# Two routing batches in place of three, the first tile's products around the last routing chain, scores in the first PSUM banks, and a thinner word-decoding schedule in the second expert

## The chip, the cores and the metric

The kernel runs on one core of a Trainium2 chip. The metric is the device time of one launch in microseconds (us); lower is better. The core has a matrix engine (PE, with its weight loads as PEld), a vector engine (DVE), an activation engine (ACT), a general engine (POOL, called GpSimd in the code) and a queue engine that issues most transfers (SP). Each engine works through its own instructions in order. PE writes to eight PSUM banks, which DVE and ACT read.

## What is computed

Sliding-window attention with four sink positions (2 sequences, 8 heads, 768 positions, width 64) gives 1536 rows of 512. A router picks two of eight experts for each row, a two-layer expert network runs on the rows of each expert, and a dense two-layer network with a sigmoid gate follows.

```python
x = attention(q, k, v)                              # 1536 x 512
noisy = x @ w_gate + log1p(exp(x @ w_noise)) * noise
top2 = the two largest of the 8 noisy logits of a row; weights = softmax of the two
out[mask] += weight * (relu(x[mask] @ w1[e]) @ w2[e])     # for each expert e
h = out @ w_in;  result = (h * sigmoid(h)) @ w_out        # w_in, w_out come as 64-bit floats
```

## The kernel before

**Numbers.** Each matrix product is made of three half-precision products (high by high, high by low, low by high). So each operand needs a high part (ACT, or POOL for the first weights) and a low part (DVE, the helper `low`, line 126).

**Attention** runs as a pipeline over steps p = 0 to 59. Steps 0 to 47 each begin the scores of a pair of heads of one block of 128 rows (four steps a block, 12 blocks); their later stages follow one to five steps behind. Work is hung on the steps by `at(step, function)`, and each engine's order is the order in which these functions are called. Per step DVE takes a maximum of the scores (`mx`, line 473) and a low part (`plo`, line 504). For each block the rows are scaled (`xs`, line 563), stored, transposed (`pm`, line 203), multiplied by the router's weights (`pl`, line 212) and copied to `lg` (line 215).

**Routing** of a batch of blocks (`noisy_top`, `route`) is a list of small steps, most of them on DVE, called the drip: a step of the attention takes one from it in its middle and one at its end, and four at its end from step 48 on. It ends in one-hot matrices `Aoh` and `Boh`, whose product (`z_part`, line 763) lists for each slot of an expert the row that goes there (`idx`, line 813). `posm` (lines 277 to 281) counts the rows ahead on PE. There are three batches: blocks 0 to 4, 5 to 8 and 9 to 11.

**The first tile.** Once the first batch is routed, the first 128 rows of expert 0 are known. They are gathered (`f_list`, line 668) and taken through expert 0 on their own: transposed (`f_xt`, line 675), first layer (`f_l1`, 24 matmuls, line 682), `f_relu`, transposed (`f_ht`, line 692), second layer (`f_l2`, 24 matmuls, line 699), out (`f_out`, line 704). The list `work` holds these as pieces, and `do_fill` runs the next ones at chosen places of the end of the attention. After `idx`, `f_gather` (line 717) fetches the other three tiles of expert 0 and `f_rows` (lines 727 and 729) transposes and splits them into `xT`.

**Experts** (`moe`): for expert e, eight pieces f of the first layer (`l1`, line 1009) alternate with the second (`l2`, line 1025). Beside them, for the next expert, rows are gathered by POOL (line 980), split (line 988) and turned by a DMA transpose on SP (`x_turn`, line 1369, one at each of f = 3 to 6 from the second expert on). `weights_step` loads and splits 512 KB weight pieces (line 877), two at each f in the second expert. `decode_step` decodes the 64-bit words of the dense network in 67 steps: an even one takes the last operation of one piece, ACT and POOL work on the next (lines 936, 937) and a load of 512 KB (line 931); an odd one stores a decoded 256 KB piece (line 962) and has two DVE operations.

Of the kernel before, what the change touches and what calls it, by code (L numbers as in the profile page):

```python
# [22 lines left out]
BATCHES = ((0, 5), (5, 9), (9, 12))  # L23
# [21 lines left out]
def setup(ctx, tc, g):  # L45
    nc = tc.nc
# [24 lines left out]
    g.iota8 = consts.tile([128, 8], F32, name="iota8")  # L71
    g.M = consts.tile([128, g.NB, 8], BF16, name="M")
    g.Msum = consts.tile([128, 8], BF16, name="Msum")
    g.top8 = consts.tile([128, g.NB, 8], F32, name="top8")
    g.ix = consts.tile([128, g.NB, 8], U32, name="ix")
    g.ef = consts.tile([128, g.NB, 2], F32, name="ef")
# [17 lines left out]
def setup_ops(tc, g):  # L94
# [3 lines left out]
    nc.gpsimd.iota(g.iota8, pattern=[[1, 8]], base=0, channel_multiplier=0,  # L98
                   allow_small_or_imprecise_dtypes=True)
    nc.gpsimd.iota(g.iotaq, pattern=[[1, 128]], base=0, channel_multiplier=0,  # L100
# [119 lines left out]
def noisy_top(tc, g, t, j0, j1):  # L220

    nc = tc.nc
    n = j1 - j0
    J = slice(j0, j1)
    V = nc.vector
    e, u, l, z, dd = (t("r" + c, [8]) for c in "eulzd")
    pre, nz = t("rp", [8]), t("rn", [8])
# [12 lines left out]
    add(lambda: V.tensor_scalar(z, u, 1.0, None, op0=OP.is_equal))  # L240
    add(lambda: V.scalar_tensor_tensor(dd, u, 1.0, z, op0=OP.subtract, op1=OP.add))
    add(lambda: V.tensor_mul(e, e, g.noise_sb[:, J, :]))
    add(lambda: V.reciprocal(dd, dd))
    add(lambda: V.tensor_mul(z, z, e))
    add(lambda: V.tensor_mul(dd, dd, e))
    add(lambda: V.tensor_add(pre, z, g.lg[:, J, 0:8]))
    add(lambda: V.tensor_mul(l, l, dd))
    add(lambda: V.tensor_add(nz, l, pre))
# [4 lines left out]
    return st  # L253


def route(tc, g, wk, ps, j0, j1):
# [6 lines left out]
    def t(name, shape, dt=F32):  # L263
# [3 lines left out]
    pos = t("rpos", [2])  # L267
    sl, pm, cl = (t(c, [2], I32) for c in ("rsl", "rpm", "rcl"))
    st = noisy_top(tc, g, t, j0, j1)
    add = st.append  # L270
    add(lambda: V.tensor_tensor(oh, g.iota8[:, None, None, :].to_broadcast([128, n, 2, 8]),
                                g.ix[:, J, 0:2, None].to_broadcast([128, n, 2, 8]), op=OP.is_equal))
    add(lambda: V.tensor_add(g.M[:, J, :], oh[:, :, 0, :], oh[:, :, 1, :]))

    def posm():
        p = ps.tile([128, n, 8], F32, name="pp", tag="M")
        nc.tensor.matmul(p, g.tri, g.M[:, J, :], start=True, stop=n == 1 and j0 == 0)
        if j0:
            nc.tensor.matmul(p, g.ones, g.Msum[:, None, :].to_broadcast([128, n, 8]), start=False, stop=n == 1)
# [5 lines left out]
        if j1 == g.NB:  # L285
            g.do_fill(4)
        V.tensor_copy(g.ef[:, J, :], g.ix[:, J, 0:2])
# [4 lines left out]
    add(lambda: V.tensor_reduce(pos, ps2, axis=AX.X, op=OP.add))  # L292

    add(lambda: V.scalar_tensor_tensor(sl, g.ef[:, J, :], 512.0, pos, op0=OP.mult, op1=OP.add))
# [12 lines left out]
    add(lambda: V.scalar_tensor_tensor(g.sl[:, J, :], g.ef[:, J, :], float(g.C), pos, op0=OP.mult, op1=OP.add))  # L307
    if j1 < g.NB:
        tot = wk.tile([128, 8], F32, name="rtot", bufs=1)

        def msum():
            V.tensor_reduce(tot, g.M[:, J, :].rearrange("p j e -> p e j"), axis=AX.X, op=OP.add)
            if j0:
                V.tensor_add(tot, tot, g.Msum)
            V.tensor_copy(g.Msum, tot)
# [5 lines left out]
def attention(tc, g):  # L321
# [4 lines left out]
    with ExitStack() as st:  # L326
# [241 lines left out]
        keep_warm(nc, g, ps, "O", 10)  # L568
# [43 lines left out]
        for n in range(NQ):  # L612
# [20 lines left out]
            if n == NQ - 1:  # L633
                at(e + 5, lambda: do_fill(2))
            at(e + 6, ga[3], "dve0")
        at(4, lambda: setup_ops(tc, g))
        for j0, j1 in g.batches:
            at(4 * j1 + (8 if j0 else 10), lambda j0=j0, j1=j1: drip.extend(route(tc, g, wk, ps, j0, j1)))
            if j0 == 0:
                at(4 * j1 + 10, lambda: drip.append(f_begin))  # L640
            if j1 == g.batches[-1][0]:
                at(4 * j1 + 8, lambda j1=j1: drip.append(lambda: z_part(0, j1)))
# [9 lines left out]
        def f_split(k, scale):  # L652
# [3 lines left out]
            nc.scalar.activation(hi, p, AF.Copy, scale=scale)  # L656
# [45 lines left out]
        def f_out():  # L702
# [6 lines left out]
        work = (fl[0] + fl[1][:2] + [lambda: f_relu(0)] + fl[1][2:] + [lambda: f_ht(0), lambda: f_relu(1)] + f2[0][:2]  # L709
                + [lambda: f_ht(1)] + f2[0][2:] + f2[1] + [f_out])  # L710
# [32 lines left out]
        g.do_fill = do_fill  # L743
# [29 lines left out]
        for p in range(NP + 12):  # L773
# [30 lines left out]
            if p == 52:  # L804
                f_xt()
            if p >= 57:
# [8 lines left out]
        do_fill(len(fill) - 5)  # L815
        f_rows(1)
        f_rows(2)
        do_fill(1)
        f_rows(3)
        do_fill(len(fill))  # L820
# [149 lines left out]
def moe(tc, g, W, wk, ps):  # L970
# [98 lines left out]
    def gates():  # L1069
# [8 lines left out]
            lambda: V.tensor_sub(e2, g.top8[:, :, 1], g.top8[:, :, 0]),  # L1078
# [68 lines left out]
    for i, (e, f) in enumerate(seq):  # L1147
# [39 lines left out]
        if i == 7:  # L1187
            dec[0][0]()
            dec[1][0]()

        for _ in range((0, 1, 1, 1, 1, 1, 2, 2)[f] + (f == 4 and e % 2) if e else 0):
# [197 lines left out]
def flag_steps(tc, g, wk, ps):  # L1389
# [3 lines left out]
    t = wk.tile([128, 5], F32, name="flt", bufs=1)  # L1393
# [3 lines left out]
    def count():  # L1397
        p = ps.tile([128, 13], F32, name="pc", tag="PT")
        nc.tensor.matmul(p[:, 0:8], g.ones, g.Msum, start=True, stop=False, skip_group_check=True)
        for j in range(g.batches[-1][0], g.NB):  # L1400
            nc.tensor.matmul(p[:, 0:8], g.ones, g.M[:, j, :], start=False, stop=False, skip_group_check=True)
        nc.tensor.matmul(p[:, 8:13], g.ones, g.over, start=False, stop=True, skip_group_check=True)
        V.tensor_reduce(t[:, 0:1], p[:, 0:8], axis=AX.X, op=OP.max)
# [6 lines left out]
            lambda: V.tensor_scalar(t[:, 0:1], t[:, 0:1], float(g.C), None, op0=OP.is_gt),  # L1410
            lambda: V.tensor_scalar(t[:, 4:5], t[:, 4:5], 0.5, None, op0=OP.is_gt),
# [28 lines left out]
def general(tc, g):  # L1440
# [4 lines left out]
    with ExitStack() as ctx:  # L1445
# [72 lines left out]
        with ExitStack() as st:  # L1518
# [15 lines left out]
            for f in noisy_top(tc, g, t, 0, NB):  # L1534
                f()
# [122 lines left out]
```

## Time and profile before

| | |
|---|---|
| median of 3 runs | 711.97 us (711.9 to 711.98) |
| profiled execution | 713.08 us, of which the span from the first to the last instruction is 711.4 us |
| mean granted TensorE clock | 0.982 of full speed |
| busy share of the span | PE 94%, DVE 60%, ACT 47%, POOL 30% |
| steps of the attention, up to the first product of expert 0 | 0 to 154.34 us |
| experts | 154.34 to about 445 us |
| dense network | to 711.4 us |

The profiled execution is 1.1 us longer than the median of the runs. Times in the text below are microseconds from the start of the span. PE is the busiest engine, so what counts is where it waits and where it ran at the lower of its two clocks.

### The profile page before, as it was taken

To read this page: it belongs to the slowest core of one execution; us is meant where nothing else is said; L and a number is where in the kernel's file an instruction comes from. 1 tells how busy PE (TensorE), PEld (TensorE's weight loads), DVE (VectorE), ACT (ScalarE), POOL (GpSimd) and SP (SyncE) were. 2 spreads that over 40 slices of the span, in tenths; PEclk is the share of its full clock that TensorE was granted. 3 is DMA by queue.
4 is the path that set the end of the run, shared out by engine and by line. 5 is a ranking of instruction groups with operands and counts; after the bars stand their busy time and mean duration, and the time that the engine had idled before them with its cause. 6 is when DMAs were issued, how large, how long until landed. Compare 5 with 4: busy or idle time off the path is not lost.

```text
span 711.4 us, 11618 instructions
## 1 busy us (share of the span) xinstructions
PE 667.1 (94%) x4292; PEld 373.1 (52%) x4292; DVE 429.3 (60%) x1091; ACT 337.8 (47%) x693; POOL 214.2 (30%) x229
## 2 busy tenths in 40 slices
PE   7999889889987999999999999899999999999993
PEld 5677667557543656565555553444444444444441
DVE  5878788737695687878797854756423344232222
ACT  4888868437663555556555441443323223222221
POOL 5868950142162162625252325222100000000000
PEclk9999999799998999999999999999999999999998
DMA  7776710539798989998894514742311011000001
GB/s 153 197 168 178 179 46 24 186 97 242 283 253 309 236 293 270 330 276 267 232 297 155 150 45 135 241 149 67 82 30 59 1 30 29 30 30 1 1 0 65
DMA packets 111682, 103.50 MB, mean 145 GB/s; under 512 B 77312, under 2 KB 77568, under 8 KB 111616
## 3 DMA queue, kind: packets, MB, share of 16 engines
q1 hardware_dynamic: 106016, 86.68, 42.4%
q0 software_dynamic: 4096, 13.11, 6.1%
q10 hardware_dynamic: 1504, 2.88, 1.1%
q8 instruction: 35, 0.57, 0.3%
q14 instruction: 31, 0.25, 0.1%
HBM read 77.29 MB, written 17.30 MB: 133 GB/s over the span
## 4 chain that ended last, share of the span: by engine, by line


## 5 line engine op out<-in xcount | busy, mean ns | idle before, releaser
L1009 PE MATMUL ph<-xT,w 128*128 128x416 f16 (+1 forms) x768 | 141.7, 335 | 8.8 <-DMA win_d<-f 6.6
L1274 PE MATMUL p<-xT,w 128*128 128x512 f16 x576 | 132.2, 379 | 2.1 <-DVE xT L1260 1.4
L1291 PE MATMUL po<-w,h 128*128 128x512 f16 x576 | 132.2, 379 | 0.0
L1025 PE MATMUL py<-h,w 128*128 128x416 f16 (+1 forms) x672 | 124.1, 331 | 3.2 <-DVE h L131 2.7
L937 POOL TENSOR_SCALAR f<-f 128x512 f32<-128x512 f32 x32 | 70.6, 2211 | 157.7 <-ACT f L936 155.6
L1009 PEld LDWEIGHTS <-w 128*128 128x128 f16 x768 | 75.4, 98 | 61.3 <-DMA win_d<-f 7.0
L1277 DVE TENSOR_TENSOR f<-p,f 128x512 f32<-128x512 f32 x48 | 33.1, 691 | 110.9 <-ACT f L1276 109.3
L1025 PEld LDWEIGHTS <-w 128*128 128x128 f16 x672 | 65.7, 98 | 52.6 <-issue 6.1
L1274 PEld LDWEIGHTS <-w 128*128 128x128 f16 x576 | 56.4, 98 | 70.1 <-issue 2.4
L1291 PEld LDWEIGHTS <-h 128*128 128x128 f16 x576 | 56.3, 98 | 67.8 <-DVE h L126 0.3
L1276 ACT ACTIVATE f<-p 128x512 f32<-128x512 f32 x48 | 28.6, 596 | 128.8 <-PE p L1274 126.5
L1012 ACT ACTIVATE h<-ph 128x416 f16<-128x416 f32 (+1 forms) x64 | 31.8, 497 | 52.0 <-PE ph L1009 51.0
L126 DVE SCALAR_TENSOR_TENSOR h<-f,h 128x512 f16<-128x512 f32 x48 | 33.2, 692 | 33.4 <-ACT h L1279 33.4
L126 DVE SCALAR_TENSOR_TENSOR w<-wst,w 128x1024 f16<-128x1024 f32 x38 | 47.2, 1245 | 8.4 <-ACT w L882 8.1
L131 DVE SCALAR_TENSOR_TENSOR h<-ph,h 128x416 f16<-128x416 f32 (+1 forms) x64 | 36.2, 566 | 24.3 <-ACT h L1012 24.3
L1279 ACT ACTIVATE h<-f 128x512 f16<-128x512 f32 x48 | 30.2, 629 | 37.8 <-DVE f L1277 37.8
L482 ACT ACTIVATE P<-pS,mx 128x260 f32<-128x260 f32 (+1 forms) x96 | 43.0, 458 | 1.9 <-DVE mx L473 1.6
L882 ACT ACTIVATE w<-wst 128x1024 f16<-128x1024 f32 x38 | 39.6, 1047 | 0.0
L126 DVE SCALAR_TENSOR_TENSOR rows<-xg,rows 128x512 f16<-128x512 f32 (+1 forms) x36 | 24.8, 688 | 24.2 <-ACT rows L988 24.1
L980 POOL DMA_INDIRECT xg<-x_d,idx x28 | 32.6, 1166 | 20.5 <-DVE topsl L121 13.5
L1064 ACT ACTIVATE yo<-tpy 128x512 f32<-128x512 f32 (+1 forms) x27 | 16.1, 595 | 45.4 <-PE tpy L1054 29.6
L126 DVE SCALAR_TENSOR_TENSOR w<-rows,w 128x1024 f16<-128x1024 f32 x26 | 31.9, 1231 | 4.4 <-ACT w L882 4.1
(254 smaller groups left out, 956.1 us busy)
## 6 DMA issues: line engine op xcount, KB each, us to landing
wst<-in_moe_w_dram SPq DMA_DIRECT2D x42, 512.0 KB
rows<-in_moe_w_dram SPq DMA_DIRECT2D x22, 512.0 KB
f<-in_moe_w_in_dram SPq DMA_DIRECT2D x16, 512.0 KB
f<-in_moe_w_out_dram SPq DMA_DIRECT2D x16, 512.0 KB
y_d<-yo SPq DMA_DIRECT2D x23, 256.0 KB
rawv<-in_v_dram SPq DMA_DIRECT2D x12, 256.0 KB
x_d<-xs SPq DMA_DIRECT2D x12, 256.0 KB
rows<-in_k_dram SPq DMA_DIRECT2D x11, 256.0 KB
```

Of the source, the lines that this page charges most:

```text
L126: nc.vector.scalar_tensor_tensor(o, x, scale, hi, op0=OP.mult, op1=OP.subtract, accum_out=sum_at(g)[:o.shape[0]] if check else None)
L131: nc.vector.scalar_tensor_tensor(o, x, 0.0, hi, op0=OP.max, op1=OP.subtract, accum_out=sum_at(g))
L482: nc.scalar.activation(Pt[n][:, h, :wd], psS[pr][:, a, :wd], AF.Exp, bias=nmx[pr][:, a:a + 1], accum_out=sm[n][:, h:h + 1])
L882: nc.scalar.activation(self.u[u][k][0][:, 2 * h:2 * h + 2, :], st["t"], AF.Copy, scale=scale)
L937: nc.gpsimd.tensor_scalar(a, a, 2.0 ** -15, 2.0 ** -80, op0=OP.max, op1=OP.mult)
L980: nc.gpsimd.indirect_dma_start(out=t[:CT[c]], out_offset=None, in_=g.x_d[:, :], in_offset=bass.IndirectOffsetOnAxis(ap=g.idx[:CT[c], 4 * e ...
L1009: nc.tensor.matmul(p[:, v], w[x][:, d, c], xT[e][y][:, d, v], start=d == 0 and k == 0, stop=d == 3 and k == 2)
L1012: nc.scalar.activation(hi[:, v], p[:, v], AF.Relu)
L1025: nc.tensor.matmul(ys[e][d][:, v], w[x][:, f % 4, d * 128:(d + 1) * 128], h[y][:, v], start=f == 0 and k == 0, stop=f == 7 and k == 2)
L1274: nc.tensor.matmul(p, w[x][:, d, c], xT[q][y][:, d, :], start=z == 0, stop=z == 11)
L1277: V.tensor_mul(s, p, s)
L1291: nc.tensor.matmul(po[q][t], h[x][:, 128 * t:128 * t + 128], w[y][:, f % 4, :], start=f == 0 and k == 0, stop=f == 15 and k == 2)
```

## The change

It does five things.

1. The routing batches become blocks 0 to 5 and 6 to 11. The first enters the drip at step 34 (it was 30), the last at step 55 (it was 56).
2. The routing is written with fewer DVE operations: the two largest logits are found for a whole batch by two reductions and comparisons, in place of a `max` and a `max_index` for each block; slot numbers start from preset counts in `Msum`; the `z` term of the logarithm goes.
3. The first tile's work moves: its list at step 48, `f_xt` at step 56, five pieces at step 57 and five at step 59, its second layer after the gathers are issued. Its first high part is taken by DVE and no longer by ACT. `f_rows` and `f_out` come last, in that order.
4. The warm-up tile takes the tag "S", so the scores' tiles get the first PSUM banks. The expert stage takes its first two banks for `ph`, the output of `l1`.
5. In the second expert `decode_step` runs once at each of f = 1 to 7 (it was 10 steps, now 7), and ten times in each later one (it was 9 or 10).

```diff
-BATCHES = ((0, 5), (5, 9), (9, 12))
+BATCHES = ((0, 6), (6, 12))
...
-    t = ps.tile([128, 4, 128], F32, name="warm", tag=tag)
+    t = ps.tile([128, 2, 512], F32, name="warm", tag=tag)[:, 0].rearrange("p (a b) -> p a b", a=4)
...
-    for j in range(n):
-        add(lambda j=j: V.max(g.top8[:, j0 + j, :], nz[:, j, :]))
-    for j in range(n):
-        add(lambda j=j: V.max_index(g.ix[:, j0 + j, :], g.top8[:, j0 + j, :], nz[:, j, :]))
...
+    def pick(k):
+        m = g.top2[:, J, k]
+        add(lambda: V.tensor_reduce(m, nz, axis=AX.X, op=OP.max))
+        add(lambda: V.tensor_tensor(oh[:, :, k, :], nz, m[:, :, None].to_broadcast([128, n, 8]), op=OP.is_equal))
+    pick(0)
+    add(lambda: V.scalar_tensor_tensor(nz, oh[:, :, 0, :], -3e38, nz, op0=OP.mult, op1=OP.add))
+    pick(1)
...
-        if j1 == g.NB:
-            g.do_fill(4)
...
-        keep_warm(nc, g, ps, "O", 10)
+        keep_warm(nc, g, ps, "S", 10)
...
-                at(e + 5, lambda: do_fill(2))
+                at(e + 7, lambda: f_xt())
+                at(e + 8, lambda: do_fill(5))
+                at(e + 10, lambda: do_fill(5))
...
-            nc.scalar.activation(hi, p, AF.Copy, scale=scale)
+            if k:
+                nc.scalar.activation(hi, p, AF.Copy, scale=scale)
+            else:
+                nc.vector.tensor_scalar(hi, p, scale, None, op0=OP.mult)
...
+        do_fill(len(fill))
+        f_ht(0)
         z_part(g.batches[-1][0], NB)
         z = zt[0]
         nc.vector.tensor_scalar(g.idx, z, float(g.N - 1), None, op0=OP.min)
         f_gather()
-        do_fill(len(fill) - 5)
+        for f in f2[0][:2] + [lambda: f_ht(1)] + f2[0][2:] + f2[1]:
+            f()
+        for f in g.after:
+            f()
         f_rows(1)
         f_rows(2)
-        do_fill(1)
         f_rows(3)
-        do_fill(len(fill))
+        f_out()
...
-        for _ in range((0, 1, 1, 1, 1, 1, 2, 2)[f] + (f == 4 and e % 2) if e else 0):
+        for _ in range(((0, 1, 1, 1, 1, 1, 1, 1), (0, 1, 1, 1, 1, 2, 2, 2))[e > 1][f] if e else 0):
             decode_step(dstep[0])
```

On PE, at the very end of the attention, these rows stood before: the transposes of two of the fetched tiles (`rawv`), then the second layer of the first tile (`pf_2744`), with the third tile's transposes nine matmuls ahead of the first product of expert 0 (`ph`, not shown here).

```order
L699 LDWEIGHTS fp_204
L699 MATMUL pf_2744<-w_377,fp_204 128x512
L727 MATMUL pf_2765<-idf,rawv 128x128 x4
L727 MATMUL pf_2772<-idf,rawv 128x128 x4
L699 LDWEIGHTS fp_203
L699 MATMUL pf_2744<-w_1136,fp_203 128x512
```

In the changed kernel, at the same place, up to the first product of expert 0:

```order
L707 LDWEIGHTS fp_202
L707 MATMUL pf_2671<-w_1135,fp_202 128x512
L734 MATMUL pf_2706<-idf,rawv 128x128 x4
L734 MATMUL pf_2713<-idf,rawv 128x128 x4
L734 MATMUL pf_2720<-idf,rawv 128x32 x4
L1016 LDWEIGHTS w_374
L1016 MATMUL ph<-xT,w_374 128x288
```

All three tiles' transposes now stand directly ahead of expert 0, with the whole second layer of the first tile before them.

On DVE, around the row list `idx`, before (`Aoh` and `Boh` are of the last batch of three blocks, `fp_204` is the low part of the first tile's hidden layer):

```order
L297 TENSOR_TENSOR Boh<-iota_118,rcl 128x192
L303 TENSOR_TENSOR Aoh<-iotaq,rpm 128x512
L303 TENSOR_TENSOR Aoh<-iotaq,rpm 128x256
L307 SCALAR_TENSOR_TENSOR sl<-ef,rpos 128x6
L813 TENSOR_SCALAR idx<-pz 128x32
L126 SCALAR_TENSOR_TENSOR fp_204,sumsl<-pf_2736,fp_203 128x4x128
```

and in the changed kernel, where the last batch has six blocks:

```order
L298 TENSOR_TENSOR Boh<-iota_116,rcl 128x384
L304 TENSOR_TENSOR Aoh<-iotaq,rpm 128x512 x3
L129 SCALAR_TENSOR_TENSOR fp_202,sumsl<-pf_2645,fp_201 128x4x128
L818 TENSOR_SCALAR idx<-pz 128x32
L129 SCALAR_TENSOR_TENSOR fp_202,sumsl<-pf_2678,fp_201 128x4x128
```

Three `Aoh` products stand where there were one and a half, and the low part of the first hidden piece now stands ahead of `idx`.

On SP, in the second expert, before: the transfers from the third transpose of rows for the third expert to the fourth (`f` are loads of 64-bit words, `win_d` stores of decoded ones, `wst` and `rows_102` loads of weights).

```order
L877 DMA wst<-in_moe_w_dram 128x2x512
L962 DMA win_d<-f_3230 128x512
L931 DMA f_3403<-in_moe_w_out_dram 128x1024
L1067 DMA y_d<-yo 128x512
L1369 DMA_TRANSPOSE xT<-rows_101 128x8x128
L877 DMA wst<-in_moe_w_dram 128x2x512
L962 DMA win_d<-f_3339 128x512
L1067 DMA y_d<-yo 32x512
L1369 DMA_TRANSPOSE xT<-rows_101 128x8x32
```

and in the changed kernel:

```order
L884 DMA wst<-in_moe_w_dram 128x2x512
L969 DMA win_d<-f_3160 128x512
L1074 DMA y_d<-yo 128x512
L1376 DMA_TRANSPOSE xT<-rows_99 128x8x128
L884 DMA wst<-in_moe_w_dram 128x2x512
L938 DMA f_3381<-in_moe_w_out_dram 128x1024
L1074 DMA y_d<-yo 32x512
L1376 DMA_TRANSPOSE xT<-rows_99 128x8x32
L884 DMA wst<-in_moe_w_dram 128x2x512
L969 DMA win_d<-f_3269 128x512
```

One load of words moved behind the third transpose, and one store of 256 KB moved behind the fourth.

## Rows read from the trace of the kernel before

**Rows 1.** The page: busy time of the engines over the span.
```profile
PE 667.1 (94%) x4292; PEld 373.1 (52%) x4292; DVE 429.3 (60%) x1091; ACT 337.8 (47%) x693; POOL 214.2 (30%) x229
```

**Rows 2.** DVE's timeline (start, duration): maxima of steps 16, 20, 28, 32, 36 and 40.
```profile
45.05 0.69 DVE L473 TENSOR_REDUCE mx<-pS 128x2 f32<-128x520 f32 x1
...
55.02 0.69 DVE L473 TENSOR_REDUCE mx<-pS 128x2 f32<-128x520 f32 x1
...
73.88 0.69 DVE L473 TENSOR_REDUCE mx<-pS 128x2 f32<-128x520 f32 x1
...
83.31 0.68 DVE L473 TENSOR_REDUCE mx<-pS 128x2 f32<-128x520 f32 x1
...
95.12 0.69 DVE L473 TENSOR_REDUCE mx<-pS 128x2 f32<-128x520 f32 x1
...
106.28 0.68 DVE L473 TENSOR_REDUCE mx<-pS 128x2 f32<-128x520 f32 x1
```

**Rows 3.** Timelines of DVE and POOL: one routing operation in two batches, and POOL's work.
```profile
86.42 0.95 DVE L242 TENSOR_TENSOR re<-re,noise_sb 128x40 f32<-128x40 f32 x1
...
137.29 0.18 DVE L242 TENSOR_TENSOR re<-re,noise_sb 128x24 f32<-128x24 f32 x1
...
86.16 1.16 POOL L374 TENSOR_TENSOR v<-rawv,v 128x512 f16<-128x512 f32 x1
```

**Rows 4.** PE's timeline at the end of the attention; brackets: idle time before, releaser.
```profile
128.01 0.48 PE L556 MATMUL pO<-Vs,skT 128*128 128x512 f32 x1
...
132.21 1.89 PE L212 MATMUL pl<-wgn,xT 128*128 128x16 f32 x8 [0.31 <-DVE rps L288]
...
136.97 3.45 PE L682 MATMUL pf<-w,fp 128*128 128x512 f16 x9
...
140.26 0.18 PE L277 MATMUL pp<-M,tri 128*128 128x24 bf16 x1
...
149.97 0.43 PE L727 MATMUL pf<-idf,rawv 32*128 32x32 f32 x4
...
154.34 3.10 PE L1009 MATMUL ph<-xT,w 128*128 128x288 f16 x24 [1.89 <-ACT Aoh L704]
```

**Rows 5.** Windows: busy us of PE, PEld, DVE, ACT, POOL, granted clock, DMA, GB/s.
```profile
130.00:132.00 2.00, 0.72 (x7) 0.23 (x6) 1.41 (x8) 1.70 (x3) 0.00 (x0) 0.50 0.87 247
...
138.00:140.00 2.00, 2.00 (x6) 0.70 (x5) 1.56 (x15) 0.27 (x1) 0.00 (x0) 0.57 0.29 107
```

**Rows 6.** ACT's timeline at the end of the attention.
```profile
124.20 1.28 ACT L238 ACT_TABLE_LOAD   x1
...
151.51 0.28 ACT L729 ACTIVATE xT<-pf 128x128 f16<-128x128 f32 x1 [1.49 <-PE pf L727]
...
153.69 0.60 ACT L704 ACTIVATE Aoh<-pf 128x512 f32<-128x512 f32 x1 [1.90 <-PE pf L699]
```

**Rows 7.** DVE's timeline: the last block's logits, the last batch's count, the row list.
```profile
134.13 0.17 DVE L215 COPY lg<-pl 128x16 f32<-128x16 f32 x1 [1.25 <-PE pl L212]
...
140.54 0.20 DVE L288 TENSOR_TENSOR rps<-roh,pp 128x48 f32<-128x48 f32 x1 [0.83 <-PE pp L281]
...
143.34 0.19 DVE L813 TENSOR_SCALAR idx<-pz 128x32 int32<-128x32 f32 x1 [0.23 <-PE pz L763]
```

**Rows 8.** PE's timeline where the third expert begins.
```profile
218.51 3.80 PE L1009 MATMUL ph<-xT,w 128*128 128x416 f16 x12 [6.64 <-DMA win_d<-f]
222.15 2.27 PE L1025 MATMUL py<-h,w 128*128 128x416 f16 x12
```

**Rows 9.** SP's timeline in the second expert: when two transfers were issued.
```profile
196.70 0.37 SPq L877 DMA_DIRECT2D rows<-in_moe_w_dram  x1
...
207.79 1.18 SPq L1369 DMA_TRANSPOSE xT<-rows  x1
```

**Rows 10.** Windows of 10 us around that wait (columns as in the windows above).
```profile
200.00:210.00 10.00, 9.39 (x60) 5.34 (x59) 9.76 (x31) 6.25 (x11) 7.27 (x6) 1.00 1.09 344
210.00:220.00 10.00, 3.36 (x16) 1.56 (x15) 6.86 (x19) 1.92 (x3) 3.02 (x2) 0.74 1.04 267
```

More of the change, by code (lines that the diff above doesn't have):

```diff
@@ L276, in posm @@
         p = ps.tile([128, n, 8], F32, name="pp", tag="M")
-        nc.tensor.matmul(p, g.tri, g.M[:, J, :], start=True, stop=n == 1 and j0 == 0)
-        if j0:
-            nc.tensor.matmul(p, g.ones, g.Msum[:, None, :].to_broadcast([128, n, 8]), start=False, stop=n == 1)
+        nc.tensor.matmul(p, g.tri, g.M[:, J, :], start=True, stop=False)
+        nc.tensor.matmul(p, g.ones, g.Msum[:, None, :].to_broadcast([128, n, 8]), start=False, stop=n == 1)
         for k in range(n - 1):
@@ L291, in route, with slots @@
     add(posm)
-    add(lambda: V.tensor_reduce(pos, ps2, axis=AX.X, op=OP.add))
-    add(lambda: V.scalar_tensor_tensor(sl, g.ef[:, J, :], 512.0, pos, op0=OP.mult, op1=OP.add))
+    def slots():
+        with nc.allow_low_precision(reason="whole numbers below 8192"):
+            V.tensor_reduce(sl, ps2, axis=AX.X, op=OP.add)
+    add(slots)
     add(lambda: V.tensor_scalar(cl, sl, 7, None, op0=OP.logical_shift_right))
@@ L306, in route @@
                                              op=OP.is_equal))
-    add(lambda: V.scalar_tensor_tensor(g.sl[:, J, :], g.ef[:, J, :], float(g.C), pos, op0=OP.mult, op1=OP.add))
+    add2 = add if j1 < g.NB else g.after.append
+    add2(lambda: V.tensor_scalar(cl, sl, 9, None, op0=OP.logical_shift_right))
+    add2(lambda: V.scalar_tensor_tensor(g.sl[:, J, :], cl, float(g.C - 512), sl, op0=OP.mult, op1=OP.add))
     if j1 < g.NB:
@@ L741, in do_fill @@
                     fill.pop(0)()
-        g.do_fill = do_fill
+        g.after = []
         at(0, lambda: heads(slice(1, 4), ("M", "O")), "dve")
@@ L1187, in moe @@
         if i == 7:
-            dec[0][0]()
-            dec[1][0]()
-        for _ in range((0, 1, 1, 1, 1, 1, 2, 2)[f] + (f == 4 and e % 2) if e else 0):
+            for n in range(2):
+                dec[n][0]()
+        for _ in range(((0, 1, 1, 1, 1, 1, 1, 1), (0, 1, 1, 1, 1, 2, 2, 2))[e > 1][f] if e else 0):
             decode_step(dstep[0])
@@ L1392, in flag_steps @@
     V = nc.vector
-    t = wk.tile([128, 5], F32, name="flt", bufs=1)
+    t = wk.tile([128, 6], F32, name="flt", bufs=1)
+    cn = wk.tile([128, 8], F32, name="flc", bufs=1)
     g.flag = g.consts.tile([128, 1], I32, name="flag")
@@ L1532, in t @@
                 return wk.tile([128, NB] + shape, F32, name="g" + name)
-            for f in noisy_top(tc, g, t, 0, NB):
-                f()
+            nz, st_ = noisy(tc, g, t, 0, NB)
+            for f in st_:
+                f()
+            top8, ix = t("top8", [8]), wk.tile([128, NB, 8], U32, name="gix")
+            for j in range(NB):
+                V.max(top8[:, j, :], nz[:, j, :])
+                V.max_index(ix[:, j, :], top8[:, j, :], nz[:, j, :])
+            iota8 = wk.tile([128, 8], F32, name="giota8")
+            nc.gpsimd.iota(iota8, pattern=[[1, 8]], base=0, channel_multiplier=0,
+                           allow_small_or_imprecise_dtypes=True)
             gt = wk.tile([128, 2, NB], F32, name="ggt")
-            V.tensor_sub(gt[:, 1], g.top8[:, :, 1], g.top8[:, :, 0])
+            V.tensor_sub(gt[:, 1], top8[:, :, 1], top8[:, :, 0])
             nc.scalar.activation(gt[:, 1], gt[:, 1], AF.Exp)
```

61 lines of the change are left out of this document (24 added, 37 removed).

## The prediction, made before the changed kernel had run

> **What bounds the kernel now.** I read the page first: PE is busy 94% of the span [rows 1], so a change can only pay where PE waits or runs at its lower clock, and what it saves there reaches the end, because after the attention PE goes on almost without gaps. The edits touch three places, and I read each by the timelines of its engines.
>
> *Steps 28 to 40 of the attention.* The maxima give the pace. Four steps take 9.97 us in an ordinary stretch (45.05 to 55.02), 9.43 from step 28, 11.81 from step 32 and 11.16 from step 36 [rows 2]. The first batch's arithmetic runs in the third of these, on DVE, while POOL splits values and weights. One multiplication of 40 elements a partition took 0.95 us there, and 0.18 us with 24 elements in the last batch, when POOL stood still [rows 3]. So the stretch pays for contention more than for work.
>
> *The end of the attention.* The last attention product starts at 128.01. The last block's logits are on DVE at 134.13 [rows 7], since the router product ran from 132.21 at the lower of PE's two clocks, 1.2 GHz, behind the second batch's count [rows 4]; the granted clock was 0.50 at 130 to 132 and came back at about 139.7 (0.57 over 138 to 140) [rows 5]. The last batch's count then waits on PE until 140.26 behind nine slow products of the first tile (3.45 us), DVE gets it at 140.54, and the row list is there at 143.34 [rows 4, 7]. Then a gather decides: the third fetched tile is transposed at 149.97, that is 6.63 us after the list. Expert 0 begins 4.37 us later, at 154.34: nine products and the eviction of the first tile's output (153.69, 0.60 us) stand ahead, and PE waited 1.89 us for that eviction, whose PSUM bank it needs [rows 4, 6].
>
> *The third expert.* PE stood 6.64 us before 218.51 and then ran twelve products in 3.80 us in place of about 2.27: the clock had fallen [rows 8]. The name in the row is a store that landed at the same time. What this product needs is the fourth row transpose, issued at 207.79 [rows 9], 10.7 us before. The DMA engines are saturated (share 1.09 and 1.04, 344 and 267 GB/s) [rows 10], and a stretch of SP without issues ends at 196.70 [rows 9], so from there 21.8 us of traffic stands ahead of that transpose.
>
> **The steps of the attention: 2.4 us.** The first batch enters four steps later, so the 1.84 us by which steps 32 to 36 exceed 9.97 go. The later steps take the chain with 25 DVE operations and not 35 (15 of the old ones are the five maxima and five index searches, the latter two instructions each, so I count this low). At 0.18 us each [rows 3] the ten are 1.8 us of DVE; as DVE is the limit for about a third of these steps I count 0.6. Table loads only move with the chain. Bounds: nothing, if the contention moves along; 3.0 (both excesses, 1.84 and 1.19) plus 1.0 at most. The Trainium skill ("SBUF — State Buffer", Who interferes with whom) says that a DVE instruction with two SBUF inputs waits out a GpSimd instruction that reads SBUF. By that rule the new chain, whose products with two inputs now fall four steps later, while POOL still splits, would pay there again; the pair 0.95 and 0.18 [rows 3] agrees, and I take it as a rival below.
>
> **The end of the attention: 2.3 us.** Times here are on the old clock, before the 2.4 us.
> - A table load of 1.28 us at 124.20 goes [rows 6], and another hidden behind the wait for the logits; but 12 list products (about 0.5 us) are put in, so the last attention product ends at about 128.3 as before. The Trainium skill ("ScalarE: Activation LUTs", What ACT_TABLE_LOAD costs) prices a switch at 1.28 us and as much again for a drain. By that the switch would be worth 2.7 us, but the row behind it starts 1.3 us after the load, and neither changes the end at 128.3.
> - The last block no longer waits for the second batch's count or the first tile's transposes: logits at about 132.3, 1.9 us earlier (the product alone takes 1.89 [rows 4]), with the lower clock still granted. No other batch is left to finish then.
> - But the last batch has six blocks, and DVE now makes the first tile's high part too (0.7 us, as a maximum over 520 elements [rows 2]; its low part as much). The exponential, a table load of 1.28, nine dependent steps of about 0.2 and the two parts put the batch's one-hot rows at 137. The count waits behind twelve products: started at 134.2, they end at 138.8 at the 0.38 each of the nine [rows 4], a little sooner if the clock returns within them as it did in the twelve from 218.51 [rows 8], later if it doesn't. I take 139.
> - From there the old chain took 2.8 us to the list (140.54 to 143.34) [rows 7]; three full one-hot products in place of one and a half add 1.0, the low part ahead of the list up to 0.9. I take a total of 4.6: list at 143.8, 0.5 later than before.
> - The gather takes 6.63 again: transposes at 150.4. Behind them come only 0.43 of PE, 0.28 of ACT and about 0.3 of DVE, 1.1 with the handovers. The second layer's 24 products fit before 150.4 at full clock: 12 with 416 columns take 2.27 [rows 8], so 24 with 512 take 5.6, from 143. ACT took the third tile 1.1 us after PE had finished it (151.51 against 150.40) [rows 4, 6], for no reason that I can see; half of this stays in. Expert 0 at 152.0 against 154.34: 2.3 us. Bounds: 0 (clock low throughout, list at 146) to 4 (clock never falls).
>
> The PSUM order has no price of its own: it takes away the wait for the eviction, whose successor is DVE's last low part, in the 1.1. The two slot operations moved behind the chain lie under the second layer.
>
> **The third expert: 1.4 us.** Ahead of the fourth transpose one 256 KB store goes: at the 305 GB/s of the two windows [rows 10] 0.9 us. The load that moves from f = 4 to f = 5 is still ahead of it. A later ACT and POOL step puts POOL's gather of the next rows (416 rows, 0.85 MB, 2.8 us at that rate) later, so less of it competes: 0 to 2.8, I take 0.5. Against that stand five small DVE and PE operations of the flag (about 0.2 each), hidden as PE waits anyway; without that cover 1.0. The half-speed products (1.5 us) stay, for the wait remains some 5 us. Bounds 0 to 8.2 (6.64 + 1.53).
>
> **Sum.** 2.4 + 2.3 + 1.4 = 6.1. The profiled execution's 713.08 becomes 707.0; it lies 1.1 above the median of 711.97, so the runs should show 705.9.
>
> **The rivals.**
> - *The contention moves with the chain* and the first term is 0: then 708.3. For it: POOL's splits go on past step 34, and steps 36 to 40 were slow before, too (11.16). Against: fewer operations with two inputs. This is the time that the SBUF rule named above gives. Chance 0.15.
> - *The end gives nothing*: the low part ahead of the list, six blocks and the low clock eat the earlier logits, and steps save 1 us: 711.97 - 1 - 1.4 = 709.6. For it: PE is idle in much of the new tail, so the clock may stay at 1.2 GHz past 140. Chance 0.07, and 0.03 more for a sum under 1.4 us, which is no change.
> - *The third expert's wait closes*: the fourth transpose lands before PE arrives, 8.2 in place of 1.4: 699.1. For it: the whole backlog from 196.70 to 218.5 grew in one expert, and three decode steps of ten leave it. Against: only 256 KB of them were ahead of that transpose. Chance 0.09.
> - *Slower: the wait moves one expert on.* The third expert now has six decode steps ahead of its fourth transpose, where it had five, and the stall there is new: 6.64 + 1.53 = 8.2 us [rows 8] against 6.1 saved, 714.1. It decides if that transpose lands over 6 us after PE arrives. Against: the fourth expert had six such steps before and nothing like this wait. Chance 0.08.
>
> **How the numbers follow.** The forecast has 0.58, with 703.5 to 708 as its own range. 700.5 to 710.5 takes in the first rival and the second, and leaves out the closed wait (0.09), the slower case (0.08) and no change (0.03), 0.2 together. About 0.2% (1.4 us) is what a measurement of this kernel can tell from no change. Faster 0.89 (forecast 0.58, and 0.15, 0.07 and 0.09 of the rivals above), same 0.03, slower 0.08.
>
> **What would show it.** Right: four steps from step 32 take about 10 us; the logits of the last block come some 4 us earlier than 134.13; `idx` to the first product of expert 0 shrinks from 11.0 us to about 8.2; the wait before the third expert shrinks to about 5 us. Wrong: steps 36 to 40 grow by what 32 to 36 lose; the count still starts near 140 on the old clock; a wait of several us at the fourth expert; or no wait at the third.

## The result, and the profile after

The changed kernel takes 703.24 us (median of four runs, 702.44 to 707.11), the kernel before beside it 711.98 (711.9 to 712.12): ratio 0.9888, 95% interval 0.9851 to 0.9925. It is faster by 8.7 us, where 6.1 were forecast. The profiled execution took 702.44 us, its span is 700.7.

The page's busy times, beside those of [rows 1]; PE is a little denser:

```profile
PE 664.4 (95%) x4297; PEld 372.5 (53%) x4297; DVE 426.8 (61%) x1035; ACT 335.4 (48%) x688; POOL 212.3 (30%) x229
```

DVE's timeline, the maxima of the steps that [rows 2] shows (16, 20, 28, 32, 36, 40):

```profile
45.56 0.69 DVE L475 TENSOR_REDUCE mx<-pS 128x2 f32<-128x520 f32 x1
...
55.90 0.69 DVE L475 TENSOR_REDUCE mx<-pS 128x2 f32<-128x520 f32 x1
...
74.79 0.69 DVE L475 TENSOR_REDUCE mx<-pS 128x2 f32<-128x520 f32 x1
...
83.25 0.69 DVE L475 TENSOR_REDUCE mx<-pS 128x2 f32<-128x520 f32 x1
...
92.59 0.69 DVE L475 TENSOR_REDUCE mx<-pS 128x2 f32<-128x520 f32 x1
...
104.06 0.69 DVE L475 TENSOR_REDUCE mx<-pS 128x2 f32<-128x520 f32 x1
```

Read the differences. From step 28 four steps take 8.46 us (9.43 before), from 32 they take 9.34 (11.81), from 36 11.47 (11.16). Up to step 24 this execution is 0.9 behind (65.85 against 64.95 for the maximum of step 24). Of the edits only the warm-up tile's tag and the preset counts lie there, and that maximum comes at 64.95 to 65.59 in the four profiles with the old front (all that lies ahead of the experts) and at 65.07 to 65.94 in eight with the new one, so I take it for the difference of one execution from another.

PE's timeline at the end of the attention, with the third expert's first products at the foot (answering [rows 4] and [rows 8]):

```profile
126.18 0.48 PE L558 MATMUL pO<-Vs,skT 128*128 128x512 f32 x1
...
128.78 1.89 PE L215 MATMUL pl<-wgn,xT 128*128 128x16 f32 x8 [0.69 <-ACT xT L210]
...
136.37 0.19 PE L279 MATMUL pp<-M,tri 128*128 128x48 bf16 x1
...
150.77 3.10 PE L1016 MATMUL ph<-xT,w 128*128 128x288 f16 x24 [2.96 <-ACT Aoh L712]
...
209.70 3.76 PE L1016 MATMUL ph<-xT,w 128*128 128x416 f16 x12 [2.09 <-issue]
```

DVE has the last logits at 130.71 and the row list at 141.07 [rows 7]:

```profile
130.71 0.17 DVE L218 COPY lg<-pl 128x16 f32<-128x16 f32 x1 [3.32 <-PE pl L215]
...
141.07 0.19 DVE L818 TENSOR_SCALAR idx<-pz 128x32 int32<-128x32 f32 x1
```

So the attention ends 1.83 us earlier, expert 0 begins 3.57 earlier (150.77 against 154.34), and the third expert 8.81 earlier (209.70 against 218.51): 5.24 us, the largest piece, come between expert 0 and the third expert, where the prediction had 1.4. The wait there is 2.09 us in place of 6.64. Behind it no expert begins with a wait of 0.3 us or more, so the stall did not move on. The last part of the two spans' 10.7 us, just under 2, comes later, most of it (1.5) in the dense network, which no edit touches; I take it for the difference of one execution from another, since the one lies above its median and the other below (713.08 against 711.98, 702.44 against 703.24).

What changed there is seen in the rows of POOL and SP. In the kernel before, POOL's gathers of the rows for the expert after next, and SP's third and fourth row transposes (the fourth, at 207.79, is in [rows 9]):

```profile
204.53 1.24 POOL L980 DMA_INDIRECT xg<-x_d,idx  x1 [0.16 <-issue]
...
208.83 0.87 POOL L980 DMA_INDIRECT xg<-x_d,idx  x1 [0.30 <-DVE f L945]
...
203.40 2.48 SPq L1369 DMA_TRANSPOSE xT<-rows  x1
```

In the changed kernel:

```profile
202.47 2.62 POOL L944 TENSOR_SCALAR f<-f 128x512 f32<-128x512 f32 x1 [6.44 <-ACT f L943]
205.25 1.03 POOL L987 DMA_INDIRECT xg<-x_d,idx  x1 [0.16 <-issue]
...
199.34 1.64 SPq L1376 DMA_TRANSPOSE xT<-rows  x1
203.13 1.18 SPq L1376 DMA_TRANSPOSE xT<-rows  x1
```

Before, the first gather is issued 3.3 us ahead of the fourth transpose; after, 2.1 us behind it, since POOL first had a decoding to wait for (6.44 us idle, then 2.62). That order, and not the 256 KB which the prediction counted, became the theory to test.

### The profile page after: what moved, and what is told of

Read it like the earlier page. It is cut to its first block, busy times and chain, and to the rows that moved or that the text cites. A ratio compares the mean times of both kernels' runs of the same rounds, so it can differ in the third digit from the quotient of the medians.

```text
span 700.7 us, 11570 instructions
## 1 busy us (share of the span) xinstructions
PE 664.4 (95%) x4297; PEld 372.5 (53%) x4297; DVE 426.8 (61%) x1035; ACT 335.4 (48%) x688; POOL 212.3 (30%) x229
## 4 chain that ended last, share of the span: by engine, by line
## 5 line engine op out<-in xcount | busy, mean ns | idle before, releaser
L129 DVE SCALAR_TENSOR_TENSOR rows<-xg,rows 128x512 f16<-128x512 f32 (+1 forms) x36 | 24.8, 688 | 26.7 <-ACT rows L995 26.6
L987 POOL DMA_INDIRECT xg<-x_d,idx x28 | 30.8, 1100 | 19.2 <-DVE topsl L124 12.2
```

What stands on the lines that cost most here:

```text
L129: nc.vector.scalar_tensor_tensor(o, x, scale, hi, op0=OP.mult, op1=OP.subtract, accum_out=sum_at(g)[:o.shape[0]] if check else None)
L987: nc.gpsimd.indirect_dma_start(out=t[:CT[c]], out_offset=None, in_=g.x_d[:, :], in_offset=bass.IndirectOffsetOnAxis(ap=g.idx[:CT[c], 4 * e ...
```

## The experiments

Every kernel was timed in five rounds beside the kernel before, in three groups of four kernels, each group on a chip of its own; the kernel before had medians of 712.33, 712.32 and 712.32 us there (708.6 to 717.5 in 53 runs). The ratio behind a time is that to the kernel before, with its 95% interval. Differences between two kernels are differences of medians; as the runs of one kernel spread over 1.2 to 8.1 us, a difference of 2 us or less between two of them is barely told from none. Each kernel has one profile.

**The schedule alone.** The kernel before with the new line of decode steps:

```diff
-        for _ in range((0, 1, 1, 1, 1, 1, 2, 2)[f] + (f == 4 and e % 2) if e else 0):
+        for _ in range(((0, 1, 1, 1, 1, 1, 1, 1), (0, 1, 1, 1, 1, 2, 2, 2))[e > 1][f] if e else 0):
```

> The kernel before with the new decode schedule and nothing else of the change. In the profiles the time from the start of expert 0 to the start of the third expert fell by 5.2 us, where the prediction had 1.4. Theory A, the schedule alone does that: PE's wait before the third expert falls from 6.64 us to 2 to 3 us, and the time by 4 to 6 us, to 706 to 708. Theory B, the prediction's price was right and the rest is that the front part comes earlier or that one run differs from another: the wait stays near 5 us and the time is 710 to 711. The attention and its end must not move: expert 0 begins within 0.5 us of 154.34.

703.64 us, ratio 0.9868 [0.9833, 0.9904]: this one line gives as much as the whole change. Its PE rows, expert 0 and third expert:

```profile
150.93 3.10 PE L1009 MATMUL ph<-xT,w 128*128 128x288 f16 x24 [0.69 <-ACT Aoh L704]
...
212.70 3.63 PE L1009 MATMUL ph<-xT,w 128*128 128x416 f16 x12 [3.45 <-DMA y_d<-yo]
```

The schedule alone does it, as theory A said, but not within its numbers: the time is below its 706 to 708, and the wait of 3.45 is above its 2 to 3. Here, too, the fourth transpose (205.85) now comes ahead of the first gather (207.06). What was not expected is the first row: with the code of before up to there, expert 0 begins at 150.93 and not at 154.34. The one profile of before that the prediction read was a late execution.

**The rest alone.** The changed kernel with the old line:

```diff
-        for _ in range(((0, 1, 1, 1, 1, 1, 1, 1), (0, 1, 1, 1, 1, 2, 2, 2))[e > 1][f] if e else 0):
+        for _ in range((0, 1, 1, 1, 1, 1, 2, 2)[f] + (f == 4 and e % 2) if e else 0):
```

> The changed kernel with the old decode schedule. Theory A, parts of the change add up: the third expert's wait is back at 6 to 7 us, the time is 4 to 6 us above the changed kernel's, 707 to 709, and expert 0 still begins near 150.8. Theory B, the schedule is worth 1.4 us: 704 to 705. Theory C, the front's 3.6 us are lost in the wait, because the transfers don't begin earlier: the wait grows to about 10 us and the time is 711 to 712.

711.19 us, ratio 0.9966 [0.9943, 0.9989]: the front parts by themselves are worth 1.1 us by the medians, and 0.8 to 4.1 by that interval. Theory A and B both fall; it is nearest to C.

```profile
149.22 3.11 PE L1016 MATMUL ph<-xT,w 128*128 128x288 f16 x24 [1.45 <-DVE xT L129]
...
215.66 4.32 PE L1016 MATMUL ph<-xT,w 128*128 128x416 f16 x12 [8.82 <-DMA win_d<-f]
```

Expert 0 begins 5.1 us earlier than in [rows 4], the third expert only 2.85: the wait grew to 8.82, and the products behind it ran in 4.32 us, at the lower clock (granted 0.50 from 215.7 to 220). The first gather comes at 199.43, 4.4 us ahead of the fourth transpose (203.81).

**The bank order.**

```diff
-    t = ps.tile([128, 2, 512], F32, name="warm", tag=tag)[:, 0].rearrange("p (a b) -> p a b", a=4)
+    t = ps.tile([128, 4, 128], F32, name="warm", tag=tag)
...
-        keep_warm(nc, g, ps, "S", 10)
+        keep_warm(nc, g, ps, "O", 10)
```

> The changed kernel with the warm-up tile back in the tag O, so that the order of the PSUM banks is the old one. The prediction gave the bank order no price of its own. Theory A, it has one: PE waits for the eviction of the first tile's output again before expert 0, which comes some 1 us later, 704 to 705. Theory B, the eviction comes right behind that of the third tile anyway (150.13 against 149.96 in the changed kernel), so nothing moves: 703 to 704, within 0.5 us of the changed kernel. The steps 0 to 24 of the attention, which took 0.9 us longer in the changed kernel's profile (maximum of step 24 at 65.85 against 64.95), tell by the way: if the bank order is the cause, that maximum is back near 64.9 here; if it is not, it stays near 65.9.

703.93 us (0.9882 [0.9843, 0.9921]), no difference that can be told from the changed kernel. Expert 0 begins at 149.03, behind DVE's low part and not behind the eviction. The maximum of step 24 is at 65.60, between the two, and at 65.56 in the schedule-only kernel, which has the old order: the 0.9 us of the early steps are not the bank order's.

**A still thinner schedule.**

```diff
-        for _ in range(((0, 1, 1, 1, 1, 1, 1, 1), (0, 1, 1, 1, 1, 2, 2, 2))[e > 1][f] if e else 0):
+        for _ in range(((0, 1, 1, 1, 1, 0, 0, 0), (0, 1, 1, 1, 2, 2, 2, 2))[e > 1][f] if e else 0):
```

> The changed kernel with four decode steps in the second expert in place of seven, at f = 1 to 4, and eleven in place of ten in each later one. Theory A, the word transfers that stand ahead of the fourth row transpose make the rest of the wait: the wait before the third expert (2.09 us, and 1.7 us of half clock behind it) goes, the time is 2 to 4 us lower than the changed kernel's, 699 to 701. Theory B, what is left of the wait is the weights' traffic: the wait stays over 1 us and the time within 1 us of the changed kernel's. Theory C, eleven steps crowd the later experts: waits for DVE of 0.5 us or a late transpose at each later expert, and the time is 1 to 4 us longer.

711.33 us, 0.9985 [0.9966, 1.0004]: nearly the whole gain is lost, twice what theory C allowed, and A and B fall. A falls in a way that points to the cause. There are fewer words in front of the fourth transpose, and yet:

```profile
213.90 4.34 PE L1016 MATMUL ph<-xT,w 128*128 128x416 f16 x12 [5.58 <-DMA xT<-rows]
...
196.89 1.09 POOL L987 DMA_INDIRECT xg<-x_d,idx  x1 [0.16 <-issue]
...
200.09 3.96 SPq L1376 DMA_TRANSPOSE xT<-rows  x1
205.46 1.18 SPq L1376 DMA_TRANSPOSE xT<-rows  x1
```

With no decoding in their way the gathers start at 196.89, in front of even the third transpose, whose issue then holds SP for 3.96 us (1.64 in the changed kernel). The later experts, with eleven steps each, lose the rest (PE waits up to 1.3 us for DVE there, as theory C said, and 1.7 us before the fifth expert): from the third expert to the dense network 231.5 us, against 224.9 in the second profile below.

**The changed kernel again**, for its spread:

> The changed kernel once more, unchanged, for a second profile and for its spread. If the profile of the first stands for the kernel, the last attention product starts near 126.2, expert 0 between 149 and 151, the wait before the third expert is 2 to 3 us, and the median is 702 to 705. What differs from the first by more than that is the difference of one execution from another and not the change's.

703.13 us (701.84 to 706.19). It begins expert 0 at 149.60, and the third expert as follows:

```profile
210.18 2.27 PE L1016 MATMUL ph<-xT,w 128*128 128x416 f16 x12 [2.15 <-DMA y_d<-yo]
```

**The gather alone.** The kernel before, old schedule, one move:

```diff
-        if f == 6 and e + 2 < E:
+        if f == (7 if e == 1 else 6) and e + 2 < E:
             gather(e + 2)
```

> The kernel before with one move: in the second expert POOL's gather of the rows that come after the next expert's is issued at f = 7 in place of f = 6, behind POOL's decoding of that piece; the decode schedule is the old one. Theory G (gathers): the 0.85 MB of these gathers, issued at 204.5 to 209.7 and so in front of the fourth row transpose issued at 207.79, are what delays that transpose; behind it they cost nothing: the wait before the third expert falls from 6.64 to 1 to 3.5 us and the time by 4 to 6 us, to 706 to 708. Theory W (words): it is the loads and stores of 64-bit words that the old schedule puts in front of the transpose; they stay where they were, so the wait stays over 5 us and the time within 1.5 us of the kernel before.

706.53 us (705.5 to 706.69), 0.9921 [0.9889, 0.9952]. Theory G holds: 5.8 us from this move.

```profile
213.21 2.27 PE L1009 MATMUL ph<-xT,w 128*128 128x416 f16 x12 [2.19 <-DMA win_d<-f]
...
210.09 1.03 POOL L980 DMA_INDIRECT xg<-x_d,idx  x1 [0.16 <-issue]
...
207.30 1.21 SPq L1369 DMA_TRANSPOSE xT<-rows  x1
```

The transpose is issued at nearly the old time (207.30 against 207.79) behind the same words, but PE starts 5.9 us after it and not 10.7, and its clock does not fall (2.27 in place of 3.80). The traffic by queue fits it. From 203 to 218 in the kernel before (packets, MB, share of the 16 DMA engines; q0 carries POOL's gathers):

```profile
q1 hardware_dynamic: 3465, 3.58, 79.0%
q0 software_dynamic: 272, 0.85, 28.4%
```

and from 203 to 213 in this kernel, where q0 has nothing:

```profile
q1 hardware_dynamic: 2905, 3.53, 107.5%
```

The same 3.5 MB of q1 pass in 10 us in place of 15. The gathers' packets took 28.4% of 15 us, 4.3 us of all engines.

**The gather put first**, in the changed kernel, by moving one of its seven steps:

```diff
-        for _ in range(((0, 1, 1, 1, 1, 1, 1, 1), (0, 1, 1, 1, 1, 2, 2, 2))[e > 1][f] if e else 0):
+        for _ in range(((0, 1, 1, 1, 1, 0, 1, 2), (0, 1, 1, 1, 1, 2, 2, 2))[e > 1][f] if e else 0):
```

> The changed kernel with one decode step of the second expert moved from f = 5 to f = 7, seven steps as before: on POOL the gathers then stand in front of the third piece's decoding and not behind it, and on SP one load of 512 KB of words goes from in front of the fourth row transpose to behind it. Theory G (gathers): the gathers start some 8 us earlier, land in front of the transpose, and the wait before the third expert grows from 2.1 to 4 to 7 us; the time is 2 to 5 us above the changed kernel's, 705 to 708. Theory W (words): there is 0.5 MB less of words in front of the transpose, so the wait goes and the time falls by 1 to 3 us.

705.91 us, 2.8 above the changed kernel's 703.13, as theory G had it; theory W had the other sign.

```profile
211.75 4.34 PE L1016 MATMUL ph<-xT,w 128*128 128x416 f16 x12 [5.84 <-DMA xT<-rows]
...
194.48 1.09 POOL L987 DMA_INDIRECT xg<-x_d,idx  x1 [0.16 <-issue]
...
197.86 4.68 SPq L1376 DMA_TRANSPOSE xT<-rows  x1
203.80 1.18 SPq L1376 DMA_TRANSPOSE xT<-rows  x1
```

In this profile, as in that of the thinner schedule, PE's wait is put down to the transpose itself (`xT<-rows`), which is what PE needs there.

**The order of the first tile's fetches.**

```diff
-            for c in range(1, 4):
+            for c in (3, 1, 2):
...
+        f_rows(3)
         f_rows(1)
         f_rows(2)
-        f_rows(3)
```

> The changed kernel with the three gathers behind the row list, and the transposes and splits of their tiles, in the order third (32 rows), first, second. In the changed kernel's profile ACT took the third tile 2.15 us after PE's last transpose of it was recorded (149.96 against 147.81), and PE waited 2.96 us for expert 0. Theory A, the late one is the gather of 32 rows, whatever its place: then it is hidden behind the other two now, the last tile is split at about 148.5, expert 0 begins near 149.3, 1 to 2 us earlier, if the execution is one of the late kind. Theory B, it is the last gather that is late, since the four gathers of the next expert's rows follow on the same queue: nothing changes, expert 0 begins at 149 to 151 as in the other profiles. Either way the time moves by less than 1.5 us, since the wait before the third expert takes up a part.

704.63 us (0.9897 [0.9863, 0.9931]); its profile shows no late tile, so neither theory was tried. All but one of the other profiles with the new front turned out to show none either. Its profiled execution, a long one of 707.2, is of use in another way: the third transpose took 3.13 us to issue there, so the fourth came at 205.42, only 0.6 us ahead of the first gather (206.05), and the wait was 5.41. In the changed kernel's two profiles the order is won by a margin of some 2 us.

**The late gather in the changed kernel.**

```diff
-        if f == 6 and e + 2 < E:
+        if f == 6 and e != 1 and e + 2 < E:
             gather(e + 2)
...
             decode_step(dstep[0])
             dstep[0] += 1
+        if f == 7 and e == 1:
+            gather(3)
```

> The changed kernel with POOL's gather of the second expert issued at the end of f = 7, behind one more piece of decoding. Theory G, its gathers stand just behind the fourth row transpose by 2 us in the changed kernel (205.7 against 203.7 in its second profile) and in some executions overtake it: moved by some 7 us they can't, so the runs no longer spread over 4 us and the median falls by 1 to 3 us, to 700 to 702, with a wait of 1 to 2 us before the third expert. Rival, the spread comes from elsewhere (the end of the attention): the median stays within 0.7 us of the changed kernel's and the spread is as wide.

701.16 us (700.49 to 703.98), 0.9851 [0.9812, 0.9891]: the fastest of all by its median, 2.0 below the changed kernel, with a spread of 3.5 us against 4.4.

```profile
208.31 2.27 PE L1016 MATMUL ph<-xT,w 128*128 128x416 f16 x12 [2.10 <-DMA y_d<-yo]
```

Gathers come from 208.36, the fourth transpose at 202.09. The median is what theory G said, but it is not shown that G is the reason: the wait is the one that the changed kernel has in its profiles (2.09 and 2.15), no profile of that kernel shows a gather overtaking, and the intervals of the two kernels overlap.

**The same with the old front**, that is the kernel before with the schedule's new line (the first diff of this section) and these lines:

```diff
-        if f == 6 and e + 2 < E:
+        if f == 6 and e != 1 and e + 2 < E:
...
+        if f == 7 and e == 1:
+            gather(3)
```

> The kernel before with the new decode schedule and the same late gather, so that it differs from the last kernel in everything of the change that lies before the experts (batches, routing operations, first tile, PSUM order). In the profiles expert 0 begins at 149.0 to 150.8 with those parts and at 150.9 to 154.3 without. Theory A, once the third expert's wait is out of the way the front parts are worth what they save up to expert 0, 2 to 3.5 us: this kernel takes 703 to 705. Theory B, the later waits swallow most of it: it takes within 1 us of the last kernel.

703.23 us (700.74 to 706.76), 0.9882 [0.9836, 0.9928]: 2.1 above the last kernel, the low end of theory A, with intervals that overlap. Its spread is 6 us, so the gather is not the only source of spread. The wait before the third expert is 2.83:

```profile
212.19 2.27 PE L1009 MATMUL ph<-xT,w 128*128 128x416 f16 x12 [2.83 <-DMA y_d<-yo]
```

**The late gather with the old schedule**, in the changed kernel: the old line again (the second diff), and

```diff
-        if f == 6 and e + 2 < E:
+        if f == (7 if e == 1 else 6) and e + 2 < E:
```

> The changed kernel with the old decode schedule, and the gather of the second expert at f = 7 as in the kernel before with that move alone (706.53). Theory G, the schedule's whole worth was to bring the gathers behind the transpose, so with the late gather the old one is nearly as good: 702 to 705, the wait at 1.5 to 3 us. Theory W, the words in front of the transpose count as well: 705 to 708, with a wait over 4 us. Against the kernel before with the same move it also gives the worth of the front parts: theory A of the last kernel says 2 to 3.5 us less than 706.53, theory B less than 1 us.

705.02 us (702.65 to 706.45), 0.9894 [0.9855, 0.9933]: the time is at the border of the two theories, the wait is theory G's.

```profile
212.23 3.78 PE L1016 MATMUL ph<-xT,w 128*128 128x416 f16 x12 [2.75 <-DMA win_d<-f]
```

The gather's move is worth 6.2 here (711.19 to 705.02). With the gather late, the new schedule is worth another 3.9 (705.02 to 701.16), and 3.3 with the old front (706.53 to 703.23): over a third of the whole. Whether that is theory W's fewer words is not shown. The fourth transpose is issued 1.6 and 2.1 us sooner after the start of expert 0, which fits it; but the wait shrinks in one pair (2.75 to 2.10) and grows in the other (2.19 to 2.83), and part of the gain lies behind the start of the third expert. The front is worth 1.5 (706.53 to 705.02).

**Three batches, with the short chain.**

```diff
-BATCHES = ((0, 6), (6, 12))
+BATCHES = ((0, 5), (5, 9), (9, 12))
```

> The changed kernel with the three old batches (blocks 0 to 4, 5 to 8, 9 to 11); the first enters the drip at step 30 again, the second and the third at steps 43 and 55. It keeps the shorter chain of routing operations. The prediction put 1.84 us on the later entry and 0.6 us on the fewer operations. Theory A, the entry decides: the four steps from step 32 take 11 us or more again (11.81 and 11.56 in the two profiles of the old front, 9.34 to 9.45 with the new one), and the last attention product starts 1 to 2 us later than 126.0. Theory B, the operations decide: the steps stay under 10 us. At the end, a third batch of three blocks has half the one-hot products, so the row list may come up to 1 us sooner against 15.4 us from the last attention product in the changed kernel, unless the second batch holds it up as it did before. Time 703 to 705.

708.28 us (0.9949 [0.9919, 0.9978]), 5.1 above the changed kernel and outside the 703 to 705 expected. DVE's maxima of steps 32 and 36:

```profile
84.52 0.69 DVE L475 TENSOR_REDUCE mx<-pS 128x2 f32<-128x520 f32 x1
...
96.72 0.68 DVE L475 TENSOR_REDUCE mx<-pS 128x2 f32<-128x520 f32 x1
```

12.20 us, more than any profile of the long chain (11.56 to 11.81): the entry decides, and the fewer operations alone bring nothing there. The last attention product came at 131.96, 4 to 5 us later than forecast for it, with the second batch's chain in the last steps; how much of that is the order of PE's work there was not taken apart.

## Why the prediction came out as it did

The total came out inside the range, just under the forecast's own 703.5 to 708, and that is in part luck: errors of opposite sign offset each other. The front, two terms priced at 4.7 us together, is worth 0.5 to 2.1 us in the runs; the schedule behind the third term, priced at 1.4, is worth 8.1 to 8.7 (711.19 to 703.13, 712.33 to 703.64). The 0.2% that a measurement was to tell from no change was too fine as well: the interval of the result reaches 0.37% to either side.

**What bounds it.** Right: what was saved was saved where PE waited, and the third expert's wait was the largest place.

**Attention, 2.4 us.** 1.83 in the two profiles, 1.7 over all (last attention product at 127.4 to 128.0 in four profiles of the old front, 125.4 to 126.2 in eight of the new, the reordered fetches and three batches left out). Steps 32 to 36 lost their excess as said. But the contention did move along in part, the first rival and the first sign of being wrong: steps 36 to 40 take 11.46 to 11.47 in seven of those eight profiles of the new front and 12.03 in one, and 10.13 to 10.20 in three of the old one (the 11.16 of [rows 2] was an execution with the lower clock, granted 0.57, at 95 to 99). So about 1.3 of the 2.3 us come back there, and 0.45 more in steps 40 to 44 (9.53 against 9.08). Against that stand 1.0 us of steps 28 to 32, a gain that I did not count. The product of [rows 3] shows the contention in the changed kernel, at 93.20 beside POOL and at 131.52 without:

```profile
93.20 0.65 DVE L243 TENSOR_TENSOR re<-re,noise_sb 128x48 f32<-128x48 f32 x1
...
93.18 0.63 POOL L374 TENSOR_SCALAR rawv<-rawv 128x512 f32<-128x512 f32 x1
...
131.52 0.20 DVE L243 TENSOR_TENSOR re<-re,noise_sb 128x48 f32<-128x48 f32 x1
```

The rule of the Trainium skill that the prediction weighed ("SBUF — State Buffer", Who interferes with whom) agrees with this pair: the product ends (93.85) just behind POOL's instruction (93.81).

**End of the attention, 2.3 us.** The mechanism was right in its steps: on the old clock, logits at 132.54 (forecast 132.3), count at 138.2 (139), list at 142.9 (143.8); from list to expert 0 8.2 was forecast, and 8.18 or 8.19 is what seven of these eight profiles show (9.70 in the first, where ACT took the third tile 2.15 us after PE's last recorded transpose). The size was off on the side of before: its 11.0 us in [rows 4, 7] were the longest of four executions, 9.62, 9.62 and 9.82 in the others. From the last attention product to expert 0 the mean falls from 24.8 to 23.7, 1.1 us. The bank order costs nothing that can be measured, as said.

**Third expert, 1.4 us. This step failed.** It reads: "A later ACT and POOL step puts POOL's gather of the next rows ... later, so less of it competes: 0 to 2.8, I take 0.5." The gather is the main cause, by itself 5.8 to 6.2 us, and the rest of the schedule 3.3 to 3.9, in part perhaps the fewer words. I had the mechanism, put its price at the bytes over the mean rate, and took a fifth of that. Its packets took 4.3 us of the engines, near the 4.45 by which the move alone shortened the wait (6.64 to 2.19), and PE's fall to the lower clock (1.53) came on top; so even the bound of 2.8 was too low. The sign that the wait shrinks to about 5 us failed for the same reason: it shrank to 2.1. Nor did traffic for 21.8 us stand ahead of the transpose: from 196.7 to 200 the share of the DMA engines was 0.62, and only from 200 were they full (1.08). It was not seen that the order of two rows, gathers at 204.53 and transpose at 207.79, was about to turn round: POOL's timeline, which was not among the rows read, shows it. The rival of the closed wait was nearer in size (8.2), though the wait did not close.

**The sum.** The terms do not add. The front brings expert 0 2.8 us forward over all profiles, and the kernel is faster by 0.5 (703.64 to 703.13 with the new schedule), 1.1 (old schedule), 1.5 and 2.1 us (late gather). With the old schedule the lost part is the longer third wait, 8.82. For the other pairs the differences lie within the spread of the runs, and where the rest goes stays open. The slower rival, a stall one expert on, shows in no profile; a wait of 1.2 us before the fifth expert stands in that of the late gather in the changed kernel, and what makes it was not tried.

## What to carry to other kernels

Where a transfer that an engine waits for shares saturated DMA engines, look at every queue for what is issued just ahead of it, and price a neighbour by the share of the engines its packets take (here 4.3 us), not by its bytes (2.8); then move the neighbour that nobody waits for, which here was one line. An edit that takes work off an engine can start such a neighbour earlier: one decode step moved from in front of the gathers cost 2.8 us. And read a second execution before a term rests on one interval of one profile.

## What was not expected of the hardware

- How long SP takes to issue one row transpose goes with the traffic: 1.24 us for the first of the four for the third expert in every profile (share of the DMA engines 0.44 from 189 to 191 in the kernel with the gather alone), 1.64 to 3.13 for the third of them (share 1.05 from 202 to 206 in the same profile) in the ten profiles where no gather had been issued by its end, 3.96 and 4.68 in the two where gathers ran from before it. The Trainium skill ("DMA: Bandwidth & Descriptors", Queues, rings and completion order) says that each DMA engine takes turns between the queues that have work, packet by packet. That q1 and q0 shared the engines above agrees with it, but no run here shows the turns.
- After nearly the same wait the clock fell to its lower level in one execution of the changed kernel and stayed at the upper in the other. Of the waits between 2 and 3 us before the third expert in all profiles, it fell after those of 2.09, 2.33 and 2.75 us and stayed after 2.10, 2.15, 2.19 and 2.83. Windows (busy time of PE, PEld, DVE, ACT and POOL, granted clock, DMA share, GB/s) of the first profile, wait 2.09 us, and of the second, 2.15:

```profile
210.00:213.00 3.00, 3.00 (x12) 1.34 (x10) 0.28 (x1) 0.00 (x0) 2.36 (x2) 0.55 1.03 398
```

```profile
210.00:213.00 3.00, 2.82 (x17) 1.60 (x18) 0.78 (x3) 0.51 (x1) 2.86 (x2) 1.00 1.05 399
```
